# Rounded three-pass query products, other banks at the end of the sixth chunk pair, and a projection weight loaded in two halves

## The chip, the cores and the metric

One core of one Trainium2 chip runs the whole program in one launch. The metric is the device time of an execution in microseconds; the kernel before took 1010.38 us (median of three runs, 1007.82 to 1011.08).

## The reference

Linear attention with positive random features, for 8 batches of 8 heads, 576 tokens of 64 dimensions and 128 features, and then a two-layer network on the 4608 tokens of 512 dimensions:

```python
def phi(x):
    proj = np.einsum('bhsd,df->bhsf', x, w_phi)
    proj = proj - np.max(np.abs(proj), axis=-1, keepdims=True)
    return np.concatenate([np.exp(proj), np.exp(-proj)], axis=-1)
q_p, k_p = phi(q), phi(k)
kv = np.einsum('bhsf,bhsd->bhfd', k_p, v)
z = np.sum(k_p, axis=2)
num = np.einsum('bhsf,bhfd->bhsd', q_p, kv)
den = np.einsum('bhsf,bhf->bhs', q_p, z)[..., None] + 1e-06
x = (num / den).transpose(0, 2, 1, 3).reshape(4608, 512)
out = np.maximum(x @ w_in, 0.0) ** 2 @ w_out          # d_ff = 2048
```

## The kernel before

**Attention.** Two heads make a pair, 32 pairs in all. The two heads' 64 dimensions lie in the lower and the upper 64 partitions of one tile, so that a product of each uses one half of TensorE's rows. The first six pairs (`EARLY`) are done in `early`; the other 26 in `visit` and `late`. One `visit(i)` holds the key projection of pair i+1 (`rows_k`, L539), the query projection of pair i (`rows_q`, L816), the short last 64 tokens and the sums over keys (`columns`: L825, L545, L601, L606), and the numerators of pair i-1 (L837). `rows_q` multiplies the projection weight, `wst`, by 512 queries of each head, in float32, one product for each head; the results go to the one-bank tiles `pn` and `pv`. VectorE or ScalarE copies them to `pt` (L260, L261); GpSimd takes the largest over the partitions (L913), VectorE subtracts it (L256), and ScalarE takes the exponentials (L918, L920).

**The weight.** `w_phi` is stored in DRAM in two column orders, the first for the queries and the first six pairs' keys, the other for the later keys (`wst_late`, `wbf_late`). One transfer, L332, brings all six blocks of 128 columns to the tile `wraw`, 384 KB, ahead of all other loads. The first product that is needed is the first pair's key projection (L539).

**The network.** The 18 chunks of 256 tokens are each multiplied by 8 blocks of 256 hidden units. Chunks 0 to 3 go one at a time (`moe`: L963 first layer, L1000 second layer). Chunks 4 to 17 go in seven pairs, `PAIRS`; each block's first layer (`step`, L1168) makes products of sums of both chunks, which VectorE adds up again (L1174). The hidden values are held as a rounded float32 part `gh` and a bfloat16 rest `gl`, and the second layer (`second`, L1000) is twelve products of 512 columns: bfloat16 `wl` by `gh`, bfloat16 `wl` by `gl`, and rounded float32 `wh` by `gh`. For the first six pairs (`MID`) the second chunk's hidden values are put away in DRAM (`put_away`) and taken back (`take_back`) when the first chunk's outputs are complete; both chunks accumulate in the two `po` banks, one chunk after the other. In the last pair, where attention is over, the products of `step` use the banks `pz` and `pp`, and the second chunk accumulates in `pn` and `pv` beside the first in `po`.

**The order.** Every step is an entry of a plan with its buffers. The order in which all engines' instructions are issued, queues of transfers included, is written out as a table of numbers, `ORDER`, one place for each entry; `WAYS` says for each entry that may run on several engines which one takes it. `Plan.order` only reads the two tables. Where the plan leaves TensorE without work in the early part, filler products (L1339) are put in.

Names in the rows: `q`, `k`, `v` tiles of inputs, `sx` a scratch tile for one user at a time, `kvs` and `ds` tiles for turned sums and denominators, `ring` the network's input, `o` the output tile, and buffer numbers behind the names.

## Time and profile before

| what | value |
|---|---|
| median of three runs | 1010.38 us (1007.82 to 1011.08) |
| profiled execution | 1012.27 us |
| its span, first to last instruction | 1010.3 us |
| TensorE busy | 992.3 us, 98% |
| VectorE busy | 808.2 us, 80% |
| ScalarE busy | 592.0 us, 59% |
| GpSimd busy | 345.9 us, 34% |
| granted TensorE clock, mean | 0.999 |

The profile names the engines PE (TensorE, with PEld its weight loads), DVE (VectorE), ACT (ScalarE), POOL (GpSimd) and SP (which issues transfers). A line such as L816 is a line of the kernel. The ends of TensorE's products are modelled from their starts, so that a row's duration is not the time in which the next one can start; that time is read from the starts of two rows that follow each other. A float32 product shows as two records, though it is one instruction of the program; a bfloat16 or rounded float32 one (also printed f32) is a single record.

### The profile page before, as it was taken

How to read it: one execution, taken by the hardware profiler on the slowest of the kernel's cores; microseconds unless marked ns; L12 is line 12 of the kernel's file. 1: busy time of each engine (PE TensorE's matmuls, PEld its weight loads, DVE VectorE, ACT ScalarE, POOL GpSimd, SP SyncE). 2: the span in 40 equal slices, each digit the busy share in tenths (PEclk: the TensorE clock that was granted, in tenths of full speed). 3: DMA queues.
4: the chain of work that ended last, by engine and by line, in shares of the span. 5: the costliest groups of instructions: out<-in, count | busy, mean ns of one | idle time of the engine just before them, and what ended most of it. 6: DMA issues, size and time to landing. Idle time of an engine off the chain costs nothing.

```text
span 1010.3 us, 19876 instructions
## 1 busy us (share of the span) xinstructions
PE 992.3 (98%) x7549; PEld 676.0 (67%) x7549; DVE 808.2 (80%) x1445; ACT 592.0 (59%) x1116; POOL 345.9 (34%) x137
## 2 busy tenths in 40 slices
PE   9989999999999999999999999999999999999998
PEld 5656666667667775676657775677566756766764
DVE  7899989998996887879889888778888875673453
ACT  6988875766555576376766774566646542441333
POOL 2452266554420153453364443531453330000000
PEclk9999999999999999999999999999999999999999
DMA  9766333454236765658576767657665656675411
GB/s 334 279 223 178 104 81 113 113 172 145 70 126 205 210 177 156 235 173 253 171 216 191 212 220 220 192 164 230 188 186 154 209 182 210 201 236 192 142 47 42
DMA packets 149543, 180.60 MB, mean 179 GB/s; under 512 B 76872, under 2 KB 97352, under 8 KB 147400
## 3 DMA queue, kind: packets, MB, share of 16 engines
q1 hardware_dynamic: 149160, 178.81, 57.8%
q8 instruction: 59, 0.97, 0.4%
q10 hardware_dynamic: 288, 0.52, 0.1%
q14 instruction: 36, 0.29, 0.1%
HBM read 137.93 MB, written 41.21 MB: 177 GB/s over the span
## 4 chain that ended last, share of the span: by engine, by line
PE 82%; DVE 6%; DMA 5%; ACT 3%; issue 2%; SPq 1%; POOL 1%; DVEq 0%; ACTq 0%; POOLq 0%
PE po L1000 32%; PE ph L1168 8%; PE ph L963 8%; PE pn L1168 5%; PE pv L1168 5%; PE pz L601 4%; PE pn L837 3%; PE pp L1168 2%; PE pn L816 2%; PE pp L539 2%; PE pv L837 2%; DMA w<-wd 1%; DVE w L1174 1%; DMA rb<-rd 1%; PE pz L606 1%
## 5 line engine op out<-in xcount | busy, mean ns | idle before, releaser
L1168 PEld LDWEIGHTS <-w 128*128 128x128 f16 x2352 | 224.6, 98 | 50.0 <-issue 21.0
L913 POOL PARTITION_ALL_REDUCE mx<-pt x52 | 116.0, 2231 | 239.3 <-DVE pt L261 96.9
L1000 PE MATMUL po<-wh,gh 128*128 128x512 f32 x544 | 174.2, 441 | 0.0
L1000 PE MATMUL po<-wl,gh 128*128 128x512 bf16 x544 | 140.6, 380 | 1.2 <-DMA gh<-gd 0.9
L1000 PE MATMUL po<-wl,gl 128*128 128x512 bf16 x544 | 139.8, 379 | 1.1 <-DVE gl L256 1.1
L934 POOL PARTITION_ALL_REDUCE rb<-rb x26 | 97.3, 3743 | 117.1 <-DVE rb L931 116.8
L1219 ACT ACTIVATE w<-w,cw 128x512 f32<-128x512 f32 x112 | 78.0, 715 | 95.5 <-DVE w L1174 95.4
L1000 PEld LDWEIGHTS po<-wh,gh 128*128 128x128 f32 x544 | 102.7, 189 | 31.4
L256 DVE TENSOR_TENSOR gl<-w,gh 128x512 bf16<-128x512 f32 x112 | 82.5, 742 | 43.5 <-ACT w L982 42.4
L934 POOL PARTITION_ALL_REDUCE ds<-ds x26 | 96.4, 3706 | 54.9 <-DVE ds L931 43.5
L980 ACT ACTIVATE gh<-w 128x512 fp32r<-128x512 f32 x112 | 69.7, 625 | 69.3 <-PE po L1000 36.6
L1000 PEld LDWEIGHTS <-gl 128*128 128x128 bf16 x576 | 56.2, 98 | 69.5 <-DVE gl L256 2.3
L1000 PEld LDWEIGHTS <-gh 128*128 128x128 bf16 x576 | 51.4, 98 | 57.9 <-issue 18.6
L963 PE MATMUL ph<-ring,w 128*128 128x256 f16 x768 | 89.4, 273 | 0.0
L1168 PE MATMUL ph<-ring,w 128*128 128x256 f16 x624 | 85.6, 273 | 2.9 <-DVE w L1174 2.4
L963 PEld LDWEIGHTS <-w 128*128 128x128 f16 x768 | 72.6, 98 | 18.3 <-issue 10.0
L1168 PE MATMUL pv<-w,w 128*128 128x256 f16 x576 | 70.8, 273 | 0.6 <-ACT pt L260 0.3
L587 DVE TRANSPOSE_TENSOR_REDUCE z<-e 128x32 f32<-128x1024 f32 x52 | 64.2, 1235 | 1.8 <-ACT e L563 1.8
L1174 DVE TENSOR_TENSOR w<-pv,w 128x512 f32<-128x512 f32 x96 | 53.1, 553 | 8.0 <-PE pv L1168 5.5
L256 DVE TENSOR_TENSOR qe<-pt,mx 128x576 f32<-128x576 f32 x52 | 48.1, 926 | 7.2 <-POOL mx L913 4.4
L561 ACT ACTIVATE e<-e 128x512 f32<-128x512 f32 x64 | 39.4, 624 | 24.7 <-DVE e L558 24.7
L929 ACT ACTIVATE pp<-qe,zc 128x576 f32<-128x576 f32 x52 | 38.4, 739 | 26.3 <-DVE rb L931 12.5
(257 smaller groups left out, 1814.7 us busy)
## 6 DMA issues: line engine op xcount, KB each, us to landing
w<-wd SPq DMA_DIRECT2D x112, 512.0 KB, 4.5
gd<-gh SPq DMA_DIRECT2D x48, 256.0 KB, 5.4
gh<-gd SPq DMA_DIRECT2D x48, 256.0 KB, 3.9
v<-in_vp_dram SPq DMA_DIRECT2D x32, 320.0 KB, 3.6
k<-in_kp_dram SPq DMA_DIRECT2D x32, 288.0 KB, 3.5
q<-in_qp_dram SPq DMA_DIRECT2D x32, 288.0 KB, 3.5
rb<-rd SPq DMA_DIRECT2D x64, 144.0 KB, 3.3
out_dram<-o SPq DMA_DIRECT2D x34, 256.0 KB, 4.3
```

Source lines behind the costliest of these rows:

```text
L256: eng.tensor_tensor(out=out_, in0=a, in1=b_, op=ALU.subtract)
L587: sums[p].append(P.add("DVE", dve_us(256 * k), lambda: V.tensor_reduce(out=col(), in_=src().rearrange("p k (b x) -> p k b x", x=32), op=AL ...
L601: PE.matmul(out=to[64 * h:64 * h + 64, 0:256], lhsT=v_at(p)[:, t, h, :], rhs=e_[2 * p + h][:, t].rearrange("p s f -> p (s f)"), start=t == ...
L837: PE.matmul(out=to[64 * h:64 * h + 64, :], lhsT=kz_[n][:, 128 * s_ + 64 * h:128 * s_ + 64 * h + 64], rhs=qe_[2 * n + h].rearrange("p (s x) ...
L913: o = P.add("POOL", par_us(S), lambda n=n, h=h: G.partition_all_reduce(mx_[n - EARLY], pt_[p][:, h, :], channels=128, reduce_op=bass_isa.R ...
L934: o = P.add("POOL", 3.6, lambda y=y: G.partition_all_reduce(y(), y(), channels=128, reduce_op=bass_isa.ReduceOp.add), [o], [home], R(RQ + ...
L963: PE.matmul(out=ph[:, j, :], lhsT=w_[f][0][:, w, t, 128 * j:128 * j + 128], rhs=at_ring(c, x, t), start=k == 0, stop=k == 3 * KT - 1)
L980: sq = P.add("ACT", act_us(512), lambda: A.activation(out=gh_[n], in_=r(), func=AF.Square), after, use + [("gh", n)], Q)
L1000: PE.matmul(out=bank(i), lhsT=x[:, j, 128 * i:128 * i + 128], rhs=w[:, j, :], start=turn + j + s == 0, stop=(turn, j, s) == (NFP - 1, 1, 2))
L1168: PE.matmul(out=to, lhsT=fl(x, *al)(k), rhs=fr(y, *ar)(k), start=n == 0, stop=n == 5)
L1174: V.tensor_tensor(out=to, in0=a, in1=b, op=ALU.add)
L1219: x = P.add("ACT", act_us(512, 1), lambda i=i: A.activation(out=r()[:, 2 * i:2 * i + 2, :], in_=r()[:, 2 * i:2 * i + 2, :], func=AF.Relu, ...
```

## The change

Three edits, and a new order for everything.

1. The query projection of the 26 late pairs is done in three passes. ScalarE or VectorE copies 512 columns of the queries to rounded float32 (`high_of`), VectorE subtracts that from the queries and stores the rest as bfloat16 (`low_of`), and the same is done once for the weight (`w_high`, `w_low`). `rows_q` adds up weight rest by upper half of the rounded queries (bfloat16), upper half of the rounded weight by the queries' rest (bfloat16), and rounded by rounded. The rounded copy takes every second buffer of `q`; the rest lies in `sx`.
2. In the sixth pair of chunks, the last that puts hidden values away, the last block uses the banks `pz` and `pp` in `step`, and the second chunk accumulates in `pn` and `pv`; its last block's hidden values are not put away. The seventh pair's first chunk goes on in `po`.
3. The transfer of `w_phi` is cut in two tiles, `wraw` (192 KB) at the start, and `wlate` (192 KB) later. Constant tiles `ones` and `mask` get a single column each, spread by a broadcast access; early pairs use `ds` where they used `kvs`, which shrinks.

```diff
-    wraw = cp.tile([128, 6 * F], F32, name="wraw")
+    wraw = cp.tile([128, 3 * F], F32, name="wraw")
+    wlate = cp.tile([128, 3 * F], F32, name="wlate")
...
+    q_at = lambda p: p if p < EARLY else 2 * p - EARLY
+    high_of = lambda p: (q_[q_at(p) + 1] if q_at(p) + 1 in q_.made else q_.shaped(q_at(p) + 1, [128, S], F32R))[:, 0:512]
+    low_of = lambda p: sx_["q", p].bitcast(BF16)[:, 0:512]
+    w_low = cp.tile([128, F], BF16, name="w_low")
+    w_high = cp.tile([128, F], F32R, name="w_high")
...
-    ld_w = P.add("SP", 0.45, lambda: SP.dma_start(wraw, w_phi), [], [], -100.0, land=1.7, xfer=1.36)
+    ld_w = P.add("SP", 0.45, lambda: SP.dma_start(wraw, w_phi[:, 0:3 * F]), [], [], -100.0, land=1.7, xfer=0.7)
+
+    def load_late():
+        SP.dma_start(wlate, w_phi[:, 3 * F:6 * F])
+
+    ld_late = P.add("SP", 0.45, load_late, [], [], 20.0, land=1.7, xfer=0.7)
...
-        q_load[p] = P.add("SP", 0.47, lambda: SP.dma_start(q_[p], qp[p]), [], [("q", p)], rank + 0.5, land=1.7, xfer=1.2)
+        q_load[p] = P.add("SP", 0.47, lambda: SP.dma_start(q_[q_at(p)], qp[p]), [], [("q", q_at(p))], rank + 0.5, land=1.7, xfer=1.2)
...
         def rows_q():
             for h in range(2):
-                PE.matmul(out=(pn_, pv_)[h]["Q", i], lhsT=wst[64 * h:64 * h + 64, :], rhs=q_[s][64 * h:64 * h + 64, 0:512],
-                          start=True, stop=True)
+                rows = slice(64 * h, 64 * h + 64)
+                upper = lambda x: x.bitcast(BF16).rearrange("p (c w) -> p c w", w=2)[:, :, 1]
+                wq, qh = w_high, high_of(s)
+                for x, (w, q) in enumerate(((w_low, upper(qh)), (upper(wq), low_of(s)), (wq, qh))):
+                    PE.matmul(out=(pn_, pv_)[h]["Q", i], lhsT=w[rows, :], rhs=q[rows, :], start=x == 0, stop=x == 2)
...
+            hi = P.add("ACT", act_us(512), lambda: split_high(lambda x, y: A.activation(out=x, in_=y, func=AF.Copy)),
+                       [q_load[s]], [("q", q_at(s)), key], rank - 2.0,
+                       other=[("DVE", 0.48, lambda: split_high(lambda x, y: V.tensor_copy(out=x, in_=y)), 4.0)])
+            lo = P.add("DVE", dve_us(512), lambda: sub(V, low_of(s), q_[q_at(s)][:, 0:512], high_of(s).bitcast(F32)),
+                       [hi], [("q", q_at(s)), key, low_key], rank - 2.0, lock=4.0)
+            v.append(P.add("PE", 0.76, rows_q, [lo] + w_split[-1:], [qn, qv, key, low_key], R(0.0), mode=ROWS))
...
-        if k < MID:
+        if k < MID - (turn == NFP - 1 and k == MID - 1):
...
-        later = [("po", po0 + 2 + i) for i in range(2)] if mid else [("pn", ("o", k)), ("pv", ("o", k))]
-        po0 += 4 if mid else 2
+        ends = k == MID - 1
+        later = [("pn", ("o", k)), ("pv", ("o", k))] if ends or not mid else [("po", po0 + 2 + i) for i in range(2)]
+        po0 += 4 if mid and not ends else 2
...
+            if ends and j == NFP - 1:
+                second(n, cs[1], v + 1, 0, 0, take_back(n, k, 0, m), m + 1.5, later)
+                n += 1
             done = step(cs, k, j, j, n, m)
             second(n, cs[0], v, j, j, done[0], m + 2.5, po)
-            if mid:
+            if ends and j == NFP - 1:
+                second(n + 1, cs[1], v + 1, j, 1, done[1], m + 3.0, later)
+            elif mid:
```

Both tables, `ORDER` and `WAYS`, are new. What that makes of the order shows at three places.

TensorE, the query projection of the second late pair. Before:

```order
L606 MATMUL pz_1616<-et_1383,v_863 64x256 x2
L816 MATMUL pn_1642<-q_1424,wraw 128x512
L816 MATMUL pv_1644<-q_1424,wraw 128x512
L963 LDWEIGHTS w_0_1237
L963 MATMUL ph_1652<-ring_0_76,w_0_1237 128x256
```

And of the change, in whose code L816, L963 and L1000 have become L843, L999 and L1036:

```order
L1036 MATMUL po_1422<-wh_773,gh_1433 128x512 x2
L843 LDWEIGHTS w_low
L843 MATMUL pn_1722<-q_1618,w_low 128x512
L843 LDWEIGHTS w_high
L843 MATMUL pn_1722<-sx_1688,w_high 128x512
L843 MATMUL pn_1722<-q_1618,w_high 128x512
L843 LDWEIGHTS w_low
L843 MATMUL pv_1726<-q_1618,w_low 128x512
L843 LDWEIGHTS w_high
L843 MATMUL pv_1726<-sx_1688,w_high 128x512
L843 MATMUL pv_1726<-q_1618,w_high 128x512
L999 LDWEIGHTS w_0_1531
```

Two instructions have become six products, three of the one head (`pn`) and then three of the other (`pv`); the projection now stands behind a product of the second layer.

VectorE, around the first maximum's subtraction of the second late pair (`qe` from `pt`). Before:

```order
L587 TENSOR_REDUCE z_2_1855<-e_1681 128x2x4x4
L256 TENSOR_TENSOR gl_1859<-r,gh_1792 128x512
L931 SCALAR_TENSOR_TENSOR rb_1863<-qe_1738,zc_1795,pp_1857 128x576
L587 TENSOR_REDUCE z_2_1855<-e_1755 128x2x4x4
L505 TENSOR_REDUCE m_2_147<-vm_1480 128x1
L256 TENSOR_TENSOR qe_1906<-pt_1810,mx_1852 128x576
```

And of the change:

```order
L941 TENSOR_REDUCE zc_1877<-kz_1528 128x4
L1010 TENSOR_SCALAR r<-ph_1812,cw 128x512
L598 TENSOR_REDUCE z_2_1884<-e_1686 128x2x4x4
L804 SCALAR_TENSOR_TENSOR ring_1736<-rb_1442,cb,ring_1736 128x384
L256 TENSOR_TENSOR sx_1913<-q_1738,q_1853 128x512
L256 TENSOR_TENSOR qe_1915<-pt_1849,mx_1886 128x576
```

The subtraction that makes the queries' rest, `sx` from the two `q` tiles (of the third late pair), is new in VectorE's queue; 26 of them are in the program.

SP, the first transfers. Before:

```order
L332 DMA wraw<-in_w_phi_dram 128x768
L531 DMA k_168<-in_kp_dram 128x576
L494 DMA v_170<-in_vp_dram 128x640
L532 DMA q_172<-in_qp_dram 128x576
L531 DMA k_174<-in_kp_dram 128x576
L390 DMA raw0i<-in_w_in_dram 128x2048
```

And of the change:

```order
L542 DMA k_170<-in_kp_dram 128x576
L338 DMA wraw<-in_w_phi_dram 128x384
L505 DMA v_173<-in_vp_dram 128x640
L543 DMA q_175<-in_qp_dram 128x576
L542 DMA k_177<-in_kp_dram 128x576
L401 DMA raw0i<-in_w_in_dram 128x2048
```

The first keys have moved ahead of the weight, which is half as large; the other half, `wlate`, is SP's 27th row.

## Rows read from the trace of the kernel before

**Rows 1.** The page: busy time of the engines, and the clock granted to TensorE.

```profile
PE 992.3 (98%) x7549; PEld 676.0 (67%) x7549; DVE 808.2 (80%) x1445; ACT 592.0 (59%) x1116; POOL 345.9 (34%) x137
...
PEclk9999999999999999999999999999999999999999
```

**Rows 2.** Busy time by stretch: PE, PEld, DVE, ACT, POOL, then clock, DMA share, GB/s.

```profile
100.00:300.00 200.00, 200.00 (x1539) 137.94 (x1536) 186.34 (x349) 129.75 (x246) 97.41 (x34) 1.00 0.41 119
...
350.00:800.00 450.00, 444.14 (x3305) 300.66 (x3302) 378.62 (x669) 280.58 (x548) 191.22 (x66) 1.00 0.68 199
```

**Rows 3.** The same stretches, for line L816 alone: PE and PEld.

```profile
100.00:300.00 200.00, 8.85 (x32) 2.44 (x32) 1.00 0.41 119
350.00:800.00 450.00, 19.45 (x68) 5.53 (x68) 1.00 0.68 199
```

**Rows 4.** Timeline of PE: start us, us, engine, line, operation.

```profile
107.61 1.16 PE L539 MATMUL pp<-wraw,k 64*128 64x128 f32 x16
108.60 0.59 PE L816 MATMUL pn<-q,wraw 64*128 64x512 f32 x1
108.61 0.59 PE L816 MATMUL pv<-q,wraw 64*128 64x512 f32 x1
109.03 0.59 PE L816 MATMUL pn<-q,wraw 64*128 64x512 f32 x1
109.04 0.59 PE L816 MATMUL pv<-q,wraw 64*128 64x512 f32 x1
109.56 0.61 PE L963 MATMUL ph<-ring,w 128*128 128x256 f16 x4
...
117.12 0.69 PE L816 MATMUL pn<-q,wraw 64*128 64x512 f32 x1
117.13 0.69 PE L816 MATMUL pv<-q,wraw 64*128 64x512 f32 x1
117.66 0.59 PE L816 MATMUL pn<-q,wraw 64*128 64x512 f32 x1
```

**Rows 5.** Timeline of PE: one product of the second layer, and the next one's start.

```profile
120.82 1.03 PE L1000 MATMUL po<-wl,gh 128*128 128x512 bf16 x4
121.68 1.03 PE L1000 MATMUL po<-wl,gl 128*128 128x512 bf16 x4
122.36 1.28 PE L1000 MATMUL po<-wh,gh 128*128 128x512 f32 x4
123.48 1.04 PE L1000 MATMUL po<-wl,gh 128*128 128x512 bf16 x4
```

**Rows 6.** Timeline of PE: early denominators, from 112.2, and from 112.75 on alone.

```profile
112.29 1.18 PE L732 MATMUL pn<-qe,kz 128*32 128x288 f32 x16
...
112.55 0.91 PE L732 MATMUL pn<-qe,kz 128*32 128x288 f32 x12
```

**Rows 7.** Groups by line: count, busy us, mean ns, idle us before and its releasers.

```profile
L256 DVE TENSOR_TENSOR gl<-w,gh 128x512 bf16<-128x512 f32 x112 | 82.5, 742 | 43.5 <-ACT w L982 42.4
...
L980 ACT ACTIVATE gh<-w 128x512 fp32r<-128x512 f32 x112 | 69.7, 625 | 69.3 <-PE po L1000 36.6 <-DMA gd<-gh 16.8 <-PE pv L1000 7.2
...
L1087 DVE CAST ring<-ring 128x512 f16<-128x512 f32 x8 | 4.4, 548 | 0.1
L983 DVE TENSOR_TENSOR w<-w 128x512 f32<-128x512 f32 x35 | 25.5, 730 | 27.3 <-ACT gh L980 27.3
L1021 DVE TENSOR_SCALAR o<-po,cc 128x512 f32<-128x512 f32 x11 | 8.8, 800 | 3.0 <-PE po L1000 3.0
```

**Rows 8.** Waits of PE: whom it waited for, us in total, times, longest.

```profile
PE ph L1168 <- DVE w L1174: 2.4, 3, 1.5
...
PE po L1000 <- DVE gl L256: 1.1, 2, 0.9
```

**Rows 9.** The page, DMA issues: KB each, median us from issue to landing.

```profile
q<-in_qp_dram SPq DMA_DIRECT2D x32, 288.0 KB, 3.5
```

**Rows 10.** Timeline from the start, SP's transfers and PE.

```profile
0.72 0.39 SPq L332 DMA_DIRECT2D wraw<-in_w_phi_dram  x1
1.18 0.41 SPq L531 DMA_DIRECT2D k<-in_kp_dram  x1
...
5.89 1.16 PE L539 MATMUL po<-wraw,k 64*128 64x128 f32 x16
...
7.78 0.37 PE L662 MATMUL ph<-wraw,q 64*128 64x128 f32 x1 [0.36 <-DMA q<-in_qp_dram]
```

**Rows 11.** DMA rate from 0 to 12 us, in 40 slices of 0.3 us.

```profile
GB/s 0 0 0 0 0 72 215 113 307 387 374 351 375 418 392 313 148 46 115 138 261 346 399 452 407 377 413 437 410 437 410 437 328 381 459 478 440 454 437 437
```

**Rows 12.** Timeline of PE where the sixth pair of chunks changes to its second chunk.

```profile
901.31 1.04 PE L1000 MATMUL po<-wl,gh 128*128 128x512 bf16 x4
902.53 1.04 PE L1000 MATMUL po<-wl,gl 128*128 128x512 bf16 x4 [0.19 <-DVE gl L256]
903.22 1.28 PE L1000 MATMUL po<-wh,gh 128*128 128x512 f32 x4
904.80 1.17 PE L1000 MATMUL po<-wl,gh 128*128 128x512 bf16 x4 [0.31 <-ACT o L1023]
905.81 1.02 PE L1000 MATMUL po<-wl,gl 128*128 128x512 bf16 x4
```

More of the change, by code (lines that the diff above doesn't have):

```diff
@@ L293, in tile_kernel @@
     n_ = tiles(ap, "n", [128, S], F32, 1)
[L294 removed]
+    ds_ = tiles(ap, "ds", [128, S], F32, 1)
     z4_ = tiles(sm, "z4", [128, 4, 18], F32, 1, EARLY)
@@ L640, in early @@
         o = P.add("PE", 1.7, ends, [o, exp_t[p]], kv, R(2.5), mode=(COLS, STRIPS))
-        first, second = copy(384, lambda: kvs_[p], lambda: pv_["s", p][:, 0:384])
-        o = P.add(*first, [o], [("pv", ("s", p)), ("kvs", p)], R(2.6), other=[second])
+        first, second = copy(384, lambda: ds_[p][:, 0:384], lambda: pv_["s", p][:, 0:384])
+        o = P.add(*first, [o], [("pv", ("s", p)), ("ds", p)], R(2.6), other=[second])
         def flip():
             for g in range(3):
-                PE.transpose(pv_["t", p][:, 128 * g:128 * g + 128], kvs_[p][:, 128 * g:128 * g + 128], ident)
-        o = P.add("PE", 0.35, flip, [o, pool_start], [("kvs", p), ("pv", ("t", p))], R(3.0))
+                PE.transpose(pv_["t", p][:, 128 * g:128 * g + 128], ds_[p][:, 128 * g:128 * g + 128], ident)
+        o = P.add("PE", 0.35, flip, [o, pool_start], [("ds", p), ("pv", ("t", p))], R(3.0))
         first, second = copy(384, lambda: kz_[p], lambda: pv_["t", p][:, 0:384])
@@ L655, in early @@
         q_to = lambda h: (pz_["q", p] if h else flat(ph_[p])) if free else pp_["qt", p][:, h, :]
-        q_use = [("pz", ("q", p)) if h else ("ph", p) for h in range(2)] if free else [("pp", ("qt", p))] * 2
+        q_use = [("pz", ("q", q_at(p))) if h else ("ph", p) for h in range(2)] if free else [("pp", ("qt", p))] * 2
         ut = lambda i: flat(pt_[p])[:, 128 * i:128 * i + 128]
@@ L667, in q_tail @@
             for h in range(2):
-                PE.matmul(out=pn_["qt", p][64 * h:64 * h + 64, 0:128], lhsT=q_[p][:, 512:576],
+                PE.matmul(out=pn_["qt", p][64 * h:64 * h + 64, 0:128], lhsT=q_[q_at(p)][:, 512:576],
                           rhs=wbf[:, 128 * h:128 * h + 128], start=True, stop=True)
@@ L806, in tile_kernel, with split_w, wq_high, wq_low @@
     pt_of, visited = {}, [None]
+    w_split = []
+    def split_w():
+        def wq_high():
+            A.activation(out=w_high, in_=wst, func=AF.Copy)
+        def wq_low():
+            sub(V, w_low, wst, w_high.bitcast(F32))
+        o = P.add("ACT", 0.31, wq_high, [ld_w], [], 10.0)
+        w_split.append(P.add("DVE", 0.29, wq_low, [o], [], 10.0, lock=4.0))
     def visit(i):
@@ L825, in columns @@
                     PE.matmul(out=pz_["a", i][c:c + 64, 64 * h:64 * h + 64], lhsT=wbf[:, 128 * h + c:128 * h + c + 64],
-                              rhs=q_[s][:, 512:576], start=True, stop=True)
+                              rhs=q_[q_at(s)][:, 512:576], start=True, stop=True)
             if k is not None:
@@ L844, in visit @@
             loads(k, rank - 4.0)
-            need += [k_load[k]]
+            need += [k_load[k], ld_late]
         if s is not None:
@@ L1288, in tile_kernel @@
         if p == EARLY:
+            split_w()
             visit(p - 1)
@@ L1324, in tile_kernel @@
         used = list(in_pair["pe"])
-        for j in range(NFP if mid else 0):
+        for j in range(1 if ends else 0, NFP - ends if mid else 0):
             o = take_back(n, k, j, m)
-            second(n, cs[1], v + 1, j, j, o, m + 1.5, later)
+            second(n, cs[1], v + 1, j, j + ends, o, m + 1.5, later)
             n += 1
```

188 lines of the change are left out of this document (95 added, 93 removed).

## The prediction, made before the changed kernel ran

> **What bounds the kernel now.** I read the page's shares first: TensorE is busy 992.3 of 1010.3 us at the full granted clock, VectorE 80%, ScalarE 59% [rows 1]. So a term counts only if it shortens TensorE's row of instructions or the few places where that row has to wait. The table by stages says where these are [rows 2]: from 100 to 300 us TensorE has no idle time at all, and in 350 to 800 it lacks 5.9 us of 450. Eight of the 26 late pairs' query products lie in the first stretch, 17 in the second [rows 3]: the counts there are 32 and 68 records, four to a pair. The second thing to see is VectorE: 186.3 of 200 us in the stretch where TensorE has no gap. It feeds TensorE without loss there, with 13.7 us to spare for eight pairs.
>
> **The query products (the large term).** A late pair's two heads are two float32 products of 512 columns. Each shows as two records, a first and a second pass. The heads use different halves of the array's rows and start 0.01 us apart; the second passes follow 0.43 us after the first (109.03 less 108.60), and the next work starts 0.53 us after that [rows 4]. So the columns take 2 x 0.43 = 0.86 us for both heads together, and the rest of the 0.96 us is the change of tiling; where other tiling also stands ahead, the first step is 0.54, so a change costs about 0.1. The changed kernel streams three single passes a head: bfloat16, bfloat16, rounded float32. The same three kinds, 512 columns each, make up the second layer's product: twelve in 123.48 - 120.82 = 2.66 us, or 0.222 each [rows 5]. If the two heads still run side by side, three cost 0.67 in place of 0.86: 0.19 to 0.2 less, and 26 x 0.195 = **5.1 us less**. With bfloat16's own step (0.86 / 4 = 0.215, the same group) for all three it is 5.6, the far end.
>
> The doubt is "side by side". Before, one instruction a head stands in the program and the heads alternate by themselves; now three of the first head stand in a row, then three of the second. If a product could start only once all products ahead of it have started, the second head's first pass would start with the first head's third. That makes five steps in a row, 5 x 0.222 = 1.11 us, 0.25 more than now, and +6.5 us over 26 pairs. The trace shows how products overtake. In the query products the second head's first pass starts before the first head's second pass, though both passes of the first head belong to the instruction ahead [rows 4]. In the early denominators four 32-column strips show the same: 16 records start at 112.29, of which the 12 that are left start at 112.55 or later, so all four strips' first passes had started before any second pass [rows 6]. [...] What it can't show is whether separate instructions of one part are held apart like the two passes of one instruction. I take three steps, and the five as a rival.
> [...]
>
> **What the new passes need.** 26 subtractions of 512 elements to bfloat16 on VectorE at 742 ns (the row of the same form) are 19.3 us. Of the 26 rounded copies 19 stand on ScalarE at 625 ns, 11.9 us; seven on VectorE at about the 548 ns of a 512-element cast, 3.8 us [rows 7]. The order gives some of it back: nine squares of 730 ns move from VectorE to ScalarE, six 800 ns stores of output go the other way, so VectorE gains about 18 us, 2%. This lies beside TensorE as long as VectorE has room: in 100 to 300 us eight subtractions and three casts, 8 x 0.74 + 3 x 0.55 = 7.6 us, go into 13.7 us of idle time [rows 2]. If it didn't fit, the products queued behind each query product would wait with it. TensorE's waits on VectorE after 300 us come to some 3.5 us now (2.4 and 1.1 are the largest sums) [rows 8]; I add **0.5 us**, with 0 and 3 as ends, the upper for the part of the 19.3 us that meets a busy VectorE.
> The query load has one buffer fewer, since the second now holds the rounded copy: it waits for the pair before to be read. A load lands 3.5 us after its issue [rows 9], and one copy and one subtraction follow, 1.4 us: 5 us. The order leaves over ten microseconds of TensorE work between the last read and the next pair's products, so this costs nothing; without that cover a late load would stop ScalarE's or VectorE's queue, and then TensorE.
>
> **The start.** The first product needs the keys and all of w_phi, 288 + 384 KB, and begins at 5.89 us after warm-up products [rows 10]. Now 192 KB of it stay back. At the 350 to 400 GB/s of those slices [rows 11] that is 0.5 us earlier at most; nothing at all if the queries' wait at 7.78 us or a later one absorbs it [rows 10]. I take **-0.3**. The late half is issued behind some 26 others and read from pair 6 on: it is hidden.
>
> **The end of the sixth pair of chunks.** Now its second chunk accumulates in the po banks and must wait until the first chunk's are stored: in 901 to 906 us three groups of four products start late. By starts they take 1.22, 1.58 and 1.01 us where 0.87, 1.12 and 0.87 are usual: 0.35 + 0.46 + 0.14 = 0.95 us [rows 12]. With pn and pv for that chunk the wait for a store goes, while the wait for VectorE's difference (the first of the three) may stay: **-0.5**, ends -0.95 and +0.3 (if pn or pv come late). One round trip through DRAM of two transfers less each way is off the path.
>
> **The new order.** The number of changes of tiling in TensorE's row goes from 183 to 188, at 0.1 us each **+0.5**, ends 0 and 0.5. Three fewer filler products fall into waits: nothing.
>
> Sum: -5.1 + 0.5 - 0.3 - 0.5 + 0.5 = **-4.9 us**. The profiled execution took 1012.27 us, 1.97 around its span, and would take 1007.4; it is 1.9 above the median of the runs shown, 1010.38, so the forecast for the median is **1005.5 us**. Own range: -5.6 - 0.5 - 0.95, with up to a microsecond of the other waits regained, gives 1002.5; -5.1 + 3 + 0.5 + 0.3 gives 1009.
>
> **The rivals.** (1) The heads run one behind the other, five steps a pair: +6.5 in place of -5.1, so +6.7 in all and **1017**. It decides as soon as a pair takes over four steps (4 x 0.222 = 0.89, against 0.86 now). For it: nothing in the trace shows three instructions of one half overtaken. Against it: rows 4 and 6. (2) The gain is given back: VectorE, 93% busy in the tightest stretch, makes TensorE wait 3 us or more there and after 350 us, or the rounded third pass costs two steps at 64 rows, as a float32 pass would: 4 x 0.22 is what it costs now. That is **1010**, from 1006 to 1013. For it: VectorE's 186 of 200 us; the rounded product also has the longest start-to-start time in rows 5, 1.12 for four. Against it: TensorE has no gap in that stretch at this load, and twelve products still take 2.66. (3) The change does not do what it says would be that the products still read the raw queries. The order shows them reading the copies, so I give it nothing.
>
> **How the numbers follow.** Forecast 0.61 (1002.5 to 1009), rival 2 0.18 (1006 to 1013), rival 1 0.21 (1015 to 1018.5). The range 1002 to 1013 leaves out rival 1, about 2 in 10; the forecast's own is 1002.5 to 1009. A measurement of this kernel tells about 0.3%, 3 us, from no change. Faster than 1007.3: most of the forecast (0.53) and the low end of rival 2 (0.05), 0.58. Same: the forecast's rest 0.07 and 0.11 of rival 2, 0.18. Slower than 1013.4: rival 1 and the top of rival 2, 0.24.
>
> **What would show it.** In the changed profile the query products' three records a head start in pairs 0.01 us apart and the next work follows 0.75 to 0.9 us after the first; with the second head starting 0.44 us late, and 1.2 us in all, rival 1 holds. TensorE still has no idle time in 100 to 300 us; waits of TensorE on the subtractions would be rival 2. The first key product starts near 5.4 us, and around 900 us no group of second-layer products waits for a store. I am wrong in size if waits that the reordering makes or removes exceed 2 us; they are the part that no row here prices.

## The result, and the profile after

The changed kernel takes **998.86 us** (median of 4 runs, 997.90 to 1001.13) beside 1009.50 us for the kernel before on the same chip: a ratio of 0.99 with a 95% interval of 0.9881 to 0.9918. A second set of six runs gave 1001.71 beside 1010.13, ratio 0.992, 0.9897 to 0.9944. So the change brings 8 to 11 us. The forecast was 1005.5 us, 4.9 less than before, with a range from 1002 to 1013: the sign was right, the size about half of what came, and the time lies under the range. The profiled execution took 1001.13 us, its span 999.3. One execution of the last kernel below (experiment 10, single transfer) took 2036.21 us beside 997.08 to 999.50 in its other four, and is left out of its time.

The page of the changed kernel, busy time and granted clock [rows 1]:

```profile
PE 985.0 (99%) x7598; PEld 677.3 (68%) x7598; DVE 814.1 (81%) x1468; ACT 603.7 (60%) x1145; POOL 342.6 (34%) x139
...
PEclk9999999999999999999999999999999999999999
```

The span fell by 11.0 us. TensorE's busy time fell by 7.3, from 992.3 to 985.0, though it has 49 records more, and the time in which it stood still by 3.7, from 18.0 to 14.3. The mean granted clock is 0.999 before and 1.000 after. So two things happened: the work got shorter, and it waits less. The forecast had the first too small (5.1 us for the products), and had next to nothing for the second: +0.5, -0.3 and -0.5 us.

The shorter work is the query products. Timeline of PE in the changed kernel (start us, us, engine, line, operation), the pair that answers to [rows 4], and one with other tiling ahead of it:

```profile
105.25 1.16 PE L550 MATMUL pp<-wlate,k 64*128 64x128 f32 x16
106.24 0.39 PE L843 MATMUL pn<-q,w_low 64*128 64x512 bf16 x1
106.25 0.39 PE L843 MATMUL pv<-q,w_low 64*128 64x512 bf16 x1
106.47 0.37 PE L843 MATMUL pn<-sx,w_high 64*128 64x512 bf16 x1
106.48 0.37 PE L843 MATMUL pv<-sx,w_high 64*128 64x512 bf16 x1
106.50 0.58 PE L843 MATMUL pn<-q,w_high 64*128 64x512 f32 x1
106.50 0.58 PE L843 MATMUL pv<-q,w_high 64*128 64x512 f32 x1
107.02 0.83 PE L999 MATMUL ph<-ring,w 128*128 128x256 f16 x6
...
164.54 0.62 PE L1036 MATMUL po<-wh,gh 128*128 128x512 f32 x2
165.10 0.40 PE L843 MATMUL pn<-q,w_low 64*128 64x512 bf16 x1
...
165.34 0.37 PE L843 MATMUL pn<-sx,w_high 64*128 64x512 bf16 x1
...
165.78 0.61 PE L550 MATMUL pp<-wlate,k 64*128 64x128 f32 x8
```

and a pair of the kernel before with other tiling ahead and the keys behind:

```profile
190.37 0.69 PE L816 MATMUL pn<-q,wraw 64*128 64x512 f32 x1
...
191.34 0.50 PE L539 MATMUL pp<-wraw,k 64*128 64x128 f32 x6
```

The heads start 0.01 us apart although three instructions of the first stand ahead of the second: side by side, so rival 1 is refuted in the trace. A pair takes 0.78 us where other tiling follows (107.02 - 106.24) and 0.68 where other tiling stands ahead and the keys follow (165.78 - 165.10). Before, these were 0.96 [rows 4] and 0.97 us (191.34 - 190.37). A first step behind other tiling took 0.54 us before in place of 0.43 [rows 4]; here it takes 0.24 in place of 0.23. Entering from another tiling has become nearly free (0.01 us); leaving for another still costs 0.1. Over the 26 pairs, first start to next work's start, the sum goes from 26.74 to 20.35 us, **6.4 less**. One pair of these, at 119.97, waited for its second bank and took 1.41, as one at 394.88 had before (1.48); in the second trace of the changed kernel none did, and the sum was 19.7.

The waits, by busy time in four stretches (columns as in [rows 2]), first of the kernel before:

```profile
0.00:110.00 110.00, 102.42 (x1109) 68.17 (x1110) 97.15 (x180) 92.20 (x166) 39.66 (x33) 1.00 0.73 252
110.00:550.00 440.00, 435.87 (x3282) 298.02 (x3282) 385.59 (x705) 273.52 (x532) 193.37 (x66) 1.00 0.55 161
550.00:612.00 62.00, 62.00 (x497) 43.95 (x493) 54.15 (x96) 44.79 (x87) 26.93 (x9) 1.00 0.66 192
612.00:990.00 378.00, 375.69 (x2597) 257.20 (x2596) 264.10 (x456) 175.06 (x323) 85.94 (x29) 1.00 0.60 183
```

and of the changed kernel:

```profile
0.00:110.00 110.00, 103.97 (x1132) 70.33 (x1136) 99.70 (x179) 94.41 (x178) 41.52 (x35) 1.00 0.73 253
110.00:550.00 440.00, 438.75 (x3379) 304.25 (x3372) 397.03 (x737) 281.06 (x553) 189.82 (x66) 1.00 0.56 163
550.00:612.00 62.00, 59.88 (x463) 41.59 (x463) 55.75 (x98) 44.19 (x86) 29.12 (x10) 1.00 0.63 201
612.00:990.00 378.00, 377.14 (x2610) 258.48 (x2607) 260.19 (x458) 182.01 (x328) 82.13 (x29) 1.00 0.58 177
```

TensorE's idle time is 7.6, 4.1, 0 and 2.3 us before, and 6.0, 1.3, 2.1 and 0.9 after: less everywhere but from 550 to 612 us, where a new wait has come. VectorE is fuller from 110 to 550 us, 397 in place of 386 us of 440, and TensorE waits less all the same. The two largest sums of [rows 8] are gone or small; two of the largest that are left, of the whole run (both lie between 550 and 612 us but for 0.3 us):

```profile
PE pv L1204 <- ACT pt L260: 1.3, 2, 1.0
...
PE pn L1204 <- ACT n L260: 1.0, 1, 1.0
```

At the end of the sixth pair of chunks the groups with the second chunk in pn and pv follow one another in 2.68 us (from 896.18 to 898.86), with no wait [rows 12]:

```profile
896.18 0.61 PE L1036 MATMUL pn<-wl,gh 128*128 128x512 bf16 x2
896.62 0.59 PE L1036 MATMUL pv<-wl,gh 128*128 128x512 bf16 x2
...
898.86 0.61 PE L1036 MATMUL pn<-wl,gh 128*128 128x512 bf16 x2
```

### The profile page after: what moved, and what is told of

Read it like the earlier page. It is cut to its first block, busy times and chain, and to the rows that moved or that the text cites. A ratio compares the mean times of both kernels' runs of the same rounds, so it can differ in the third digit from the quotient of the medians.

```text
span 999.3 us, 20042 instructions
## 1 busy us (share of the span) xinstructions
PE 985.0 (99%) x7598; PEld 677.3 (68%) x7598; DVE 814.1 (81%) x1468; ACT 603.7 (60%) x1145; POOL 342.6 (34%) x139
## 4 chain that ended last, share of the span: by engine, by line
PE 80%; DVE 7%; DMA 5%; ACT 4%; issue 2%; SPq 1%; POOL 0%; DVEq 0%; ACTq 0%; POOLq 0%
PE po L1036 29%; PE ph L1204 9%; PE ph L999 8%; PE pv L1204 5%; PE pn L1204 5%; PE pz L612 3%; PE pn L863 3%; PE pp L1204 2%; PE pn L1036 2%; PE pv L1036 2%; PE pp L550 2%; PE pv L863 2%; DVE w L1210 2%; PE pn L843 2%; DMA k<-in_kp_dram 1%
## 5 line engine op out<-in xcount | busy, mean ns | idle before, releaser
L970 POOL PARTITION_ALL_REDUCE rb<-rb x26 | 94.1, 3621 | 211.6 <-DVE rb L967 190.1
L1036 PE MATMUL po<-wh,gh 128*128 128x512 f32 x512 | 163.9, 441 | 0.0
L1036 PE MATMUL po<-wl,gh 128*128 128x512 bf16 x512 | 132.2, 380 | 0.0
L1036 PE MATMUL po<-wl,gl 128*128 128x512 bf16 x512 | 131.6, 379 | 0.0
L1036 PEld LDWEIGHTS po<-wh,gh 128*128 128x128 f32 x512 | 96.7, 189 | 29.5
L1036 PEld LDWEIGHTS <-gl 128*128 128x128 bf16 x576 | 56.4, 98 | 68.0
L999 PE MATMUL ph<-ring,w 128*128 128x256 f16 x768 | 89.4, 273 | 1.3 <-DVE r L1010 1.1
L1036 PEld LDWEIGHTS <-gh 128*128 128x128 bf16 x576 | 51.2, 98 | 54.4 <-issue 16.1
L999 PEld LDWEIGHTS <-w 128*128 128x128 f16 x768 | 72.8, 98 | 18.1 <-issue 8.4
L1018 ACT ACTIVATE w<-w 128x512 f32<-128x512 f32 x86 | 53.0, 623 | 0.9
L612 PE MATMUL pz<-e,v 128*64 128x256 f32 x416 | 49.3, 379 | 0.0
```

Of the source, the lines that this page charges most:

```text
L612: PE.matmul(out=to[64 * h:64 * h + 64, 0:256], lhsT=v_at(p)[:, t, h, :], rhs=e_[2 * p + h][:, t].rearrange("p s f -> p (s f)"), start=t == ...
L970: o = P.add("POOL", 3.6, lambda y=y: G.partition_all_reduce(y(), y(), channels=128, reduce_op=bass_isa.ReduceOp.add), [o], [home], R(RQ + ...
L999: PE.matmul(out=ph[:, j, :], lhsT=w_[f][0][:, w, t, 128 * j:128 * j + 128], rhs=at_ring(c, x, t), start=k == 0, stop=k == 3 * KT - 1)
L1018: o = P.add("ACT", act_us(512), lambda: A.activation(out=r(), in_=r(), func=AF.Square), [sq], use, Q, other=[("DVE", 0.70, lambda: V.tenso ...
L1036: PE.matmul(out=bank(i), lhsT=x[:, j, 128 * i:128 * i + 128], rhs=w[:, j, :], start=turn + j + s == 0, stop=(turn, j, s) == (NFP - 1, 1, 2))
```

## The experiments

The letters of the theories hold for one run each. The changed kernel's 998.86 and 1001.71 us are the base; three of its variants below that change nothing of weight lie at 1000.8, so about 1000.5 is what they are compared with. Kernels that ran beside different runs of the kernel before are compared by their ratios to it: the changed kernel's are 0.9900 and 0.9920, those of the three variants 0.9903 to 0.9918. Differences of about 3 us are near what the runs can tell.

**1. The query products alone.** Float32 products again, with the copies and subtractions gone (the lines that take them out are left out here), all else as changed:

```
-for x, (w, q) in enumerate(((w_low, upper(qh)), (upper(wq), low_of(s)), (wq, qh))):
-    PE.matmul(out=(pn_, pv_)[h]["Q", i], lhsT=w[rows, :], rhs=q[rows, :], start=x == 0, stop=x == 2)
+PE.matmul(out=(pn_, pv_)[h]["Q", i], lhsT=wst[64 * h:64 * h + 64, :], rhs=q_[q_at(s)][64 * h:64 * h + 64, 0:512],
+          start=True, stop=True)
```

> The changed kernel and its order, with the query products in float32 as before and without the copies and subtractions that the three passes need; the output is the reference's. Theory A (the passes themselves carry their part): the trace of the changed kernel has 20.4 us of query products in place of 26.7, so this run takes 6.4 us more than the changed kernel, 1005 to 1006. Rival B (the new order carries the gain, and the passes are lost in waits): at most 2 us more, up to 1001. Rival C (the added VectorE and ScalarE work makes TensorE wait, which its removal gives back): +6.4 less what the copies cost, 1001 to 1004.

Measured 1007.60 us, ratio to before 0.9966 (0.9948 to 0.9984), 6 to 9 us over the changed kernel, a little more than Theory A had; its query products sum to 27.85 us, 7.5 more than the changed kernel's (one pair waits for a bank in each). So the products carry some two thirds of the gain, and 2 to 4 us remain without them.

**2. The same, with copies and subtractions kept** (made, and read by nobody):

> The same with the copies and subtractions left in, so that only the products are float32 again. Theory A (the copies are covered): within 1 us of the run without them. Rival C (they cost): slower than the run without them by 2 us or more.

1005.54 us, ratio 0.9951 (0.9931 to 0.9970): not slower than experiment 1, the intervals overlap. The 26 copies and 26 subtractions are covered.

**3. One transfer of w_phi.**

```
-wraw = cp.tile([128, 3 * F], F32, name="wraw")
-wlate = cp.tile([128, 3 * F], F32, name="wlate")
+wraw = cp.tile([128, 6 * F], F32, name="wraw")
+wlate = wraw[:, 3 * F:6 * F]
...
-SP.dma_start(wraw, w_phi[:, 0:3 * F])
+SP.dma_start(wraw, w_phi)
```

> w_phi comes in one transfer at the start again; all else is as in the changed kernel, its order too. Theory S (the split transfer is what the start gained, and something more along the first 100 us): the first key product starts 0.5 us later, the first late query product, at 106.2 us now, at 108.5 to 110, and the time is 2 to 4 us over the changed kernel, 1001 to 1003. Theory P (my prediction's price): 0.3 to 0.5 us over it, 999.2, which five rounds can hardly tell from no change; the loss of 3.7 us by 110 us in the kernel with all three parts undone then came from chance waits of that kernel.

1000.86 us, ratio 0.9908 (0.9876 to 0.9940): no difference that can be told. Yet its first late query product starts at 109.08 us in place of 106.24. Not all of these 2.8 us are the transfer's. In this trace TensorE waits 2.0 us for VectorE until 58.83 us, and the granted clock is 0.58 from 60 to 64 us, by estimate some 1.7 us of work (0.42 of these 4 us); the trace of the changed kernel has 1.00 there:

```profile
60.00:64.00 4.00, 4.00 (x61) 2.43 (x57) 2.17 (x3) 2.00 (x3) 2.18 (x3) 0.58 0.00 1
```

Kernels with a single transfer whose granted clock is 1.00 up to 110 us reach that product at 107.68 and 107.08 us (experiments 6 and 10), 1.5 and 1.8 us behind the same kernels with the split one (106.21 and 105.28). At the query product of 573 us the changed kernel and this one are level (573.17 and 573.30): the changed kernel lost 0.65 us in the pair at 119.97 that waited for its bank, 1.0 us at 566.50 in a wait for a ScalarE copy, and the rest in smaller pieces. Experiments 9 and 10 show one more such place.

**4. The po banks for the sixth pair's second chunk again**, its first product behind the first chunk's last (the lines that count the banks and move that product are left out here):

```
-later = [("pn", ("o", k)), ("pv", ("o", k))] if ends or not mid else [("po", po0 + 2 + i) for i in range(2)]
+later = [("pn", ("o", k)), ("pv", ("o", k))] if not mid else [("po", po0 + 2 + i) for i in range(2)]
```

> Only the second chunk of the sixth pair goes back to the po banks (its first second-layer product behind the first chunk's last); all else as in the changed kernel. Theory B (what the banks alone cost under this order): in the stretch from 880 to 930 us TensorE waits 6 to 10 us more for stores, and the time is 1005 to 1009. Theory P (my prediction's price, taken from the groups that started late before): 0.5 to 0.95 us more, 999.4 to 999.8, and the remaining loss of the kernel with all three undone is from the other parts or from their acting together.

1008.61 us, ratio 0.9990 (0.9969 to 1.0012), 7 to 10 us over the changed kernel: the time is Theory B's. Its waits of PE from 880 to 935 us begin with

```profile
PE pp L1219 <- ACT w L1110: 3.1, 1, 3.1
PE po L1051 <- DVE o L1072: 1.1, 1, 1.1
PE pp L1219 <- DVE w L271: 1.0, 1, 1.0
```

In this stretch TensorE stands idle 6.5 us in place of 0.6, and behind the longest of these waits its products follow each other at about half the pace: fourteen of 256 columns take 2.89 us from 900.68 us, 0.206 each, where the changed kernel's eighteen take 1.96 from 902.85, 0.109 each. That is by estimate some 1.4 us more (fourteen times the difference; the granted clock of this span is 0.998, the changed kernel's 1.000): together about the 7.5 us by which the two spans differ (1006.8 and 999.3). The banks cost that much only under an order that was made for other banks; the order before had 0.95 us at this place [rows 12]. So this run does not say what the edit brought; that is the difference between the two traces.

**5. All three undone under the new order** (edits of 1, 3 and 4):

> All three edits undone at once, under the changed kernel's order: float32 query products without copies, the weight in a single transfer at the start, and the second chunk of the sixth pair in the po banks (its first product is moved behind the first chunk's last one; one trip of hidden values through DRAM stays left out). Theory A (about 4 us of the gain come from the new order alone, as waits that it avoids in the first 100 us and from 350 to 800 us): 1005 to 1008, clearly under the kernel before. Rival B' (the order alone gives nothing, the edits all): 1009 to 1010, as the kernel before.

1017.63 us, ratio 1.0082 (1.0057 to 1.0106), higher than either theory: 10 us over experiment 1, about what experiment 4 lost to the banks. Its trace, of its slowest execution (1021.22 us), has the same waits from 880 to 935 us, and a mean granted clock of 0.993 over its span, where experiment 1's has 1.000. An order of the work is worth its time only with the buffers that it was made for.

**6. What is left without products and transfer** (edits of 1 and 3): the new order and the banks.

> Float32 query products without copies and subtractions, and w_phi in a single transfer: of the change only the new order and the banks of the sixth pair's second chunk are left. Theory O (the gain beside the query products comes from the order, which waits less): 1006 to 1009, 1 to 4 us under the kernel before, and about the same as with the split transfer (1007.6). Theory T (it comes from the split transfer): 1010 to 1012, no gain on the kernel before. In both the first late query product starts near 109 to 110 us, in place of 106.2 with the split transfer; what differs is whether the difference is still there after 580 us.

1007.92 us, ratio 0.9980 (0.9965 to 0.9994), level with experiment 1: Theory O. Its first late query product starts at 107.68 us, earlier than both theories had it. Two of its stretches beside the four above:

```profile
110.00:550.00 440.00, 437.00 (x3294) 297.73 (x3293) 389.98 (x708) 271.14 (x532) 187.61 (x66) 1.00 0.54 160
...
612.00:990.00 378.00, 377.29 (x2608) 257.70 (x2607) 255.84 (x452) 179.99 (x326) 84.94 (x29) 1.00 0.59 181
```

3.0 and 0.7 us idle, where the kernel before has 4.1 and 2.3, with the same float32 products. The order and the banks take these waits away by themselves; how much of the second is the banks' this run does not tell (0.5 us of the 2.3 stood at the end of the sixth pair before [rows 12]). No run has the three passes under the order before, so the products' part is known only under the new one.

**7. The load on VectorE, doubled and halved.** First each copy and each subtraction twice:

```
+copy(high_of(s), q_[q_at(s)][:, 0:512])
...
-lambda: sub(V, low_of(s), q_[q_at(s)][:, 0:512], high_of(s).bitcast(F32))
+lambda: [sub(V, low_of(s), q_[q_at(s)][:, 0:512], high_of(s).bitcast(F32)) for _ in range(2)]
```

> Each late pair's rounded copy and each subtraction is issued twice, 26 x (0.62 or 0.55) us on ScalarE or VectorE and 26 x 0.74 = 19.3 us on VectorE more; all else as in the changed kernel. Theory A (this work lies in VectorE's idle time): TensorE still shows no idle time between 100 and 300 us, and the time is up to 1.5 us longer, 999 to 1000.5. Theory V (VectorE is so nearly full that its load comes through): 8 x 0.74 + 3 x 0.55 = 7.6 us go into the 16.5 us that VectorE has idle from 100 to 300 us, and where they meet dense work TensorE waits: 4 to 10 us longer, 1003 to 1009.

1018.63 us, ratio 1.0084 (1.0054 to 1.0115), 17 to 20 us more: above even Theory V's 1009. VectorE has 26.6 us more work (840.7 against 814.1), and from 110 to 550 us TensorE stands idle 9.6 us:

```profile
110.00:550.00 440.00, 430.39 (x3277) 295.74 (x3276) 406.07 (x741) 280.46 (x550) 187.30 (x65) 1.00 0.53 158
```

Then the subtractions left out, the second pass reading the rounded copy:

```
-for x, (w, q) in enumerate(((w_low, upper(qh)), (upper(wq), low_of(s)), (wq, qh))):
+for x, (w, q) in enumerate(((w_low, upper(qh)), (upper(wq), upper(qh)), (wq, qh))):
...
-lambda: sub(V, low_of(s), q_[q_at(s)][:, 0:512], high_of(s).bitcast(F32))
+lambda: None
```

> The 26 subtractions on VectorE are left out, and the second pass reads the rounded copy in place of the low part, so that the query's low part is left out of the result. TensorE's work is the same; VectorE has 26 x 0.74 = 19.3 us less. Theory A (my prediction: VectorE has room for one set of copies and subtractions): within 1 us of the changed kernel, 998 to 1000. Theory V (VectorE's load still holds TensorE back in the changed kernel, as its doubling cost some 15 to 19 us): the waits at 566 and 581 us go, TensorE is never late after 100 us, 3 to 8 us less, 991 to 996.

1000.80 us, ratio 0.9918 (0.9892 to 0.9945): no gain, Theory A. One set of copies and subtractions costs nothing, the second costs most of its own duration. Whether by VectorE's time or by the longer chain from load to product, these runs don't part; the waits are spread over many lines.

**8. How far products overtake.** Passes outside, heads inside, so that the heads alternate in the program:

```
-for h in range(2):
-    for x, (w, q) in enumerate(((w_low, upper(qh)), (upper(wq), low_of(s)), (wq, qh))):
+for x, (w, q) in enumerate(((w_low, upper(qh)), (upper(wq), low_of(s)), (wq, qh))):
+    for h in range(2):
```

> The query products' three passes are written with the pass outside and the head inside, so that the heads alternate in the program; all else as in the changed kernel. Theory A (products of another half of the rows start past the ones ahead, as far as three): nothing changes in a pair, 0.68 to 0.78 us from its first start to the next work's, total 20 to 20.5 us over 26 pairs, and the time is within 1 us of the changed kernel, 998 to 1000. Theory F (the overtaking costs something that the records do not show, or happens only where the second bank is free): the pair that took 1.41 us loses its wait and pairs take 0.67, 1 to 3 us less, 996 to 998.

1000.78 us, ratio 0.9903 (0.9870 to 0.9936), 20.25 us for the 26 pairs: the same. The pair at the second place waited again (1.39 us): that wait is for the pv bank, which a ScalarE copy was still reading (in the changed kernel's first trace the copy runs from 120.17 to 120.57 us, and the second head starts at 120.62), not for the first head. Theory A. Then the three passes four times per head, twelve and twelve:

> Each head's three passes are issued four times over, twelve products of one head ahead of twelve of the other; each repetition starts its sum afresh, so the result stays. Theory A (each half of the array has a queue of its own, deep enough): the second head's first product starts within 0.05 us of the first head's, a pair takes 12 x 0.217 + 0.1 = 2.7 us in place of 0.78, and the run about 50 us more than the changed kernel, 1049. Rival (products start in program order, or a window of a few instructions): the second head starts late, up to 11 x 0.217 = 2.4 us, a pair takes up to 5.1 us, and the run up to 113 us more, 1112.

1097.65 us (one run), between the two cases: the second head starts 1.83 us late, after nine of the first head's twelve products.

```profile
106.89 0.39 PE L843 MATMUL pn<-q,w_low 64*128 64x512 bf16 x1
...
108.53 0.57 PE L843 MATMUL pn<-q,w_high 64*128 64x512 f32 x1
108.72 0.40 PE L843 MATMUL pv<-q,w_low 64*128 64x512 bf16 x1
108.95 0.40 PE L843 MATMUL pn<-q,w_low 64*128 64x512 bf16 x1
```

And twice per head, six and six:

> Each head's three passes are issued twice, six products of the first head and then six of the second; all else as in the changed kernel. With twelve a head the second head had started 1.83 us late, after nine of the first head's twelve. Theory W (a product starts past waiting products of the other half, as long as no more than three of them still wait): the second head starts after three of the first head's six, 0.65 to 0.7 us late, a pair takes 3 + 6 steps, 2.0 to 2.2 us, and the kernel some 26 x 1.35 = 35 us longer, 1032 to 1037. Theory Q (it may start past a quarter of what waits, or after a fixed time of 1.8 us): 1.0 us late or after all six, 2.4 to 2.8 us a pair, 1042 to 1053.

1026.13 us (one run), under both. Timeline of PE of this kernel:

```profile
106.65 0.39 PE L843 MATMUL pn<-q,w_low 64*128 64x512 bf16 x1
106.88 0.37 PE L843 MATMUL pn<-sx,w_high 64*128 64x512 bf16 x1
106.90 0.58 PE L843 MATMUL pn<-q,w_high 64*128 64x512 f32 x1
107.10 0.40 PE L843 MATMUL pv<-q,w_low 64*128 64x512 bf16 x1
107.33 0.40 PE L843 MATMUL pn<-q,w_low 64*128 64x512 bf16 x1
```

The second head starts after exactly three of the first head's six. Theory W's count fits both kernels: three of the first head's products, of six and of twelve, had still to start when the second head's first one did. Its price was too high: 0.45 us are two even steps of 0.227 us and 1.83 are eight, so the second head starts with the third and the ninth product, not a step behind them. In both kernels the three that still wait are also the first head's last whole sum of three passes, and have their weight loads beside them; whether products, sums or instructions count these two do not tell. In the changed kernel two still wait when the second head starts, 0.01 us after the first.

**9. Where the early lead is lost.** The changed kernel once more, for its second trace:

> The changed kernel once more, as the base of this call. Both theories: the same time, 998 to 1001. Its second trace tells how far the first 110 us vary by themselves: the first late query product started at 106.24 us in the first trace, and at 106.2 to 108.2 in four other kernels whose first 100 us are nearly the same. Theory S (the split transfer sets it): 106 to 107 again. Theory C (chance waits of some 2 us set it): anywhere up to 109.

The first late query product starts at 105.83 us, just under what Theory S said; over all kernels with the split transfer it lies between 105.3 and 108.2, so chance has its part too, as Theory C has it. The time, 1001.71 us, is 0.7 above what was expected. And at 579 us TensorE waits 2.1 us. SyncE's queue, ScalarE and TensorE of this trace there:

```profile
564.14 0.48 SPq L972 DMA_DIRECT2D den<-ds  x1
...
565.35 0.42 SPq L1134 DMA_DIRECT2D w<-wd  x1
565.86 0.40 SPq L1136 DMA_DIRECT2D w<-wd  x1
567.00 0.33 SPq L543 DMA_DIRECT2D q<-in_qp_dram  x1
567.43 0.38 SPq L1266 DMA_DIRECT2D gd<-gh  x1
...
574.16 0.63 ACT L1016 ACTIVATE gh<-w 128x512 fp32r<-128x512 f32 x1 [4.80 <-DMA gd<-gh]
...
579.32 2.60 PE L1204 MATMUL pv<-w,w 128*128 128x256 f16 x12 [2.07 <-ACT pt L260]
```

The store of gh is issued at 567.43, behind two weight loads and a query load; ScalarE waits 4.8 us for it, and the copy queued behind on ScalarE comes late for TensorE. In this trace the granted clock behind the wait is 0.57 from 579 to 583 us: the twelve products behind it take 2.4 us from their first start to the next one's, where the first trace has 1.3, and by estimate the stretch costs some 1.7 us more (0.43 of 4 us).

```profile
579.00:583.00 4.00, 3.68 (x19) 2.60 (x19) 3.97 (x8) 3.58 (x9) 0.82 (x1) 0.57 0.46 150
```

Against the kernel of experiment 3 this trace is 3.3 us ahead up to 457 us, 2.5 at 571, and 0.4 behind at 610, though that kernel waits 1.8 us at this place too, at a clock of 1.00. In the first trace the same wait is 1.0 us, and the clock is 1.00 from 550 to 612 us.

**10. That one store ahead of the three loads**, one number of the order (the entry issues the stores of gh and of its rest gl, and both move); and the same with a single transfer of w_phi:

```
+place[2817] = 2336.5
```

Its place was 2350; the three loads stand at 2337, 2339 and 2348.

> In the changed kernel ScalarE waits 3.5 to 4.8 us near 575 us for the store of a second-layer input (gd<-gh), which SyncE issues behind two weight loads and a query load; TensorE then waits 1 to 2 us for the copy queued behind it on ScalarE. Here that one store is issued ahead of the three loads; all else as in the changed kernel. Theory D (the place where an early lead is lost again is this store): ScalarE's wait there falls under 2.5 us, TensorE waits under 0.3 us between 550 and 600 us, and the time is 1 to 2.5 us under the changed kernel, 998 to 999.5 beside 1000.5. Theory X (something else is late next, as VectorE's work for the next products): TensorE's waits between 550 and 612 us stay at 2 us, the time at 1000 to 1001.

> The same store moved ahead, and w_phi in one transfer again. Theory D: what the split transfer gains early, 2 to 3 us at the first late query product, now reaches the end: 1000 to 1002, 1.5 to 3 us over the kernel that has only the store moved. Theory X: the lead is lost elsewhere too, and both take the same time within 1 us.

997.37 us, ratio 0.9889 (0.9868 to 0.9910), and 998.1 with the single transfer (median of four), 0.9889 (0.9869 to 0.9908). TensorE, here with the split transfer, no longer waits in this stretch:

```profile
550.00:612.00 62.00, 61.74 (x472) 42.74 (x474) 56.76 (x101) 44.13 (x85) 30.11 (x11) 1.00 0.63 195
```

The waits are Theory D's: ScalarE no longer waits for the store, and TensorE stands idle 0.3 us in place of 2.1 and 2.6. In the two traces the split transfer leads by 1.8 us at the first late query product (105.28 and 107.08), still by 1.95 at the last (766.88 and 768.83), and by 2.1 in the span (994.7 and 996.8). The times of the two kernels do not show that: they are within 1 us, as Theory X had it, and the second lies under Theory D's 1000 to 1002. The first of the two is the fastest kernel of the study. By the ratios it is 1 to 3 us under the changed one, and the intervals overlap, so that the gain is shown in the traces and not by the times.

## Why the prediction fell short, step by step

**The query products: mechanism right, term too small.** The step of this term that failed is "a change costs about 0.1", charged alike in both kernels. The forecast took three steps of 0.222 against 0.86 us and let the changes cancel, 0.195 a pair. Only a pair with the keys ahead of it saves that (0.96 to 0.78). A pair behind other tiling saves 0.29 (0.97 to 0.68), since of the 0.11 us that the float32 products lost on entry [rows 4] the three passes lose 0.01. Measured: -6.4 us in the first trace, -7.0 in the second, in place of -5.1, beyond the far end of 5.6. Why entry is free for the passes no run here shows.

**Side by side or one behind the other.** Rival 1, at 0.21, was refuted: 25 of the 26 pairs have their heads within 0.13 us. In every such pair the second head's first product starts before the second and third of the first head that stand ahead of it in the program. The forecast's reading of passes that interleave was the right evidence; that behind six and twelve products the second head starts 0.45 and 1.83 us late was not in it.

**Waits on VectorE and ScalarE: +0.5 forecast, and the waits fell.** Rival 2, the gain given back, failed in the trace, in experiment 2 (copies and subtractions kept for nobody cost nothing) and in the second run of experiment 7 (leaving the subtractions out gains nothing). But the first run of experiment 7 shows how near it was: one more dose costs 17 to 20 us. "93% busy" was a fair warning, not a bound. The load itself was mis-summed: the forecast's own terms give VectorE 19.3 + 3.8 - 6.6 + 4.8 = 21.3 us more, not 18, and it measured 5.9 more (814.1 against 808.2), and from 100 to 300 us 183.5 in place of 186.3. The new subtractions and casts are there, 19.0 and 3.6 us; but the 52 subtractions of the maximum take 760 ns each in place of 926, 8.6 us less. So the copies did not have to fit into the 13.7 us alone. Why those subtractions are shorter under the new order no run here tests.

**The new order: the step that failed most.** The forecast priced only its changes of tiling, +0.5, and put the rest at nothing, saying that no row priced the waits it makes or removes. With the old products, and with the sixth pair's other banks, it removes 1.1 us of TensorE's idle time from 110 to 550 us and 1.6 from 612 to 990 (experiment 6), 2.2 to 3.4 us of time in all (1007.92 beside 1010.13, and 1007.60 beside 1010.95 in experiment 1). The trace had the rows: 6.4 us of TensorE's idle time after 110 us stood there, as 2.4 and 1.1 us in [rows 8] alone. A table that is written anew can take away any of it, so -6 belonged in the range as an end.

**The start.** -0.3 for the first product was about right: the main part of the first key product starts at 5.45 us in place of 5.89 [rows 10], with the short last part now ahead of it:

```profile
4.83 0.70 PE L556 MATMUL pn<-wraw,k 128*64 128x128 f32 x4
5.45 1.16 PE L550 MATMUL po<-wraw,k 64*128 64x128 f32 x16
```

With the single transfer under the new order it starts at 5.59 to 5.83 (experiments 3, 6 and 10), 0.1 to 0.4 us later. What the split grows to by 110 us was not foreseen: 1.5 and 1.8 us in the two comparisons at a clock of 1.00. Split transfers reach the first late query product between 105.3 and 108.2 us in the traces of this study, single ones under the same order at 107.1 and 107.7, and at 109.1 and 109.9 in experiments 3 and 5, where the granted clock was lower (0.58 from 60 to 64 us, and 0.993 over the span); so chance waits are of the same size. Nor was it foreseen that the changed kernel loses this lead again, at 120 and 566 us in one trace and near 579 us in the other.

**The end of the sixth pair.** The 0.95 us are gone, the low end of the term. A wait of 0.6 us for VectorE's w is new at 907.5 us, in the seventh pair; if it belongs to this edit, which no run here shows, the net is -0.35 where -0.5 was forecast.

```profile
907.54 0.83 PE L1204 MATMUL pp<-ring,w 128*128 128x256 f16 x6 [0.60 <-DVE w L1210]
```

**The sum.** -6.4 for the products and -3.7 for the waits, the start's and part of the sixth pair's among them, make -10.1 of the 11.0 us of span; 0.45 of the rest are groups of the sixth pair that ran late without being listed as idle. Beside the forecast's -4.9 the products were short by 1.3 and the waits, -0.3 in its terms, by 3.4; its +0.5 for changes of tiling is not seen apart.

## What to carry to other kernels

When an order of work is replaced as a whole, put the idle time that the bound engine now shows into the range as a possible gain, and look for what each long wait hangs on: here one DMA store, three places too late in a queue, made TensorE wait 1 to 2 us, and in one trace the granted clock was 0.57 for 4 us behind that wait, by estimate 1.7 us more. Price a replaced instruction by pairs of starts in the same surroundings, with other tiling ahead and behind apart, rather than by subtracting one price of a change from all. And with an engine as busy as VectorE here (186.3 of 200 us before), the first addition may be free and the second cost most of its length (17 to 20 of 26.6 us).

## What the runs showed of the hardware

- With the query products of the two heads on different halves of the array's rows, and the first head's all ahead in the program, the second head's first product started 0.01 us behind the first head's first of three (0.13 in one pair, 0.65 in one that waited for its bank), 0.45 us behind the first of six, after three of them, and 1.83 us behind the first of twelve, after nine. Seen with sums of three passes only.
- Two float32 products of 512 columns on 64 rows side by side take 0.96 us with one change of tiling; three single passes each, two bfloat16 and one rounded float32, take 0.68 with the change ahead and 0.78 with it behind.
- The rounded float32 pass on 64 rows costs, by estimate, about what a bfloat16 pass does here: 0.68 us for three passes of both heads are 0.227 a step, and bfloat16 products alone take 0.86 / 4 = 0.215 [rows 5].
- In five traces TensorE's granted clock was lower for a stretch: 0.58 from 60 to 64 us in experiment 3, 0.57 from 579 to 583 us in experiment 9, 0.97 from 550 to 612 us in the second run of 7; its mean over the whole span was 0.998 in experiment 4 and 0.993 in 5, beside 1.000 in the changed kernel's first trace. In experiments 3, 4 and 9 a wait of TensorE of 2.0, 3.1 and 2.1 us stands just ahead of the slow stretch. The first run of 7, with 9.6 us of idle time between 110 and 550 us, has 1.00 in all four stretches. Whether the waits bring the lower clock about no run tests.
